# The first 13 rows of an output weight come in six loads by partition instead of being part of one

## The chip, the cores and the metric

The kernel runs on one core of a Trainium2 chip. The time is the device time of one execution in microseconds (us); lower is better. The kernel before takes 183.64 us, the median of three runs (183.59 to 183.73). The profile is of one execution more, which took 183.48 us.

A core has four computing engines, each with its own program: TensorE (PE in the profile), VectorE (DVE), ScalarE (ACT) and GpSimd (POOL). SyncE (SP) here issues nearly all transfers. A transfer between HBM, the chip's large memory, and SBUF, the working memory of 128 partitions, is carried by up to sixteen DMA engines; each of them works through its own queue in order and adds one to the transfer's semaphore when its share has landed. TensorE writes its sums to PSUM.

## The reference

The kernel computes one step of attention for 32 sequences with a cache, and the output projection:

```python
W = min(4096, max(256, Sk // 4))          # 512 of 2048 cached positions
rep = Hq // Hkv                           # 32 query heads, 8 cached heads: 4
q = (x @ wq).reshape(B, Sq, Hq, Dh).transpose(0, 2, 1, 3)
k = jnp.repeat(k_cache[:, :, Sk - W:, :], rep, axis=1)
v = jnp.repeat(v_cache[:, :, Sk - W:, :], rep, axis=1)
scores = jnp.einsum("bhqd,bhkd->bhqk", q, k) * (Dh ** -0.5)
p = _softmax(scores, axis=-1)
o = jnp.einsum("bhqk,bhkd->bhqd", p, v)
return o.transpose(0, 2, 1, 3).reshape(B, Sq, Hq * Dh) @ wo
```

Here B is 32, D is 512, Dh is 128 and Sq is 1; all values are bf16. The last product has a left side of 32 by 4096 and takes wo, 4096 by 512, which is 4 MiB.

## The kernel before, in words

The 32 sequences are taken four at a time, in eight groups (q = 0 to 7). A group's keys and values are 4 MiB each, so with wq and wo the kernel loads 18 times 4 MiB, and a little x. All the loads of 4 MiB or of its pieces are issued by SP in the order of the list `LOADS`: K is a group's keys, V a group's values (V5 to V7 in two pieces), W a part of wo. SP issues a load as soon as the buffer it fills is free: it waits on the counters that the engines raise after each operation (`op_sem`). The loads then stand in the queues of the DMA engines in that order. wq is issued ahead of the list (L203) and x by ScalarE (L199), in loads of 25, 5 and 2 rows (`X_PARTS`).

For each group VectorE turns the keys (L506, the buffer `K_sb` to `KT_sb`), TensorE forms the scores (`scores`, L341), VectorE and ScalarE the softmax, TensorE the transposed weights (`to_value_rows`, L355) and the products with the values (`pv`, L367), and `fold` (L377) with a copy by ScalarE (L566) puts a group's result in `o_sel`. The order of operations on each engine is written out by hand (`HEAD_OPS`, `BODY_OPS`, `TAIL_OPS`), and TensorE runs the middle as a loop. The two key buffers and the two value buffers alternate.

wo is loaded last, into the first key buffer, which is free once the keys of group 6 are turned (SP's wait for `ends["T", NQ - 2, 1]`). `wo_sb` has 128 partitions of 32 rows: partition p holds the rows 32 p to 32 p + 31 of wo, 512 values each, 1 KiB a row. `WOP` cuts the 32 rows into three loads, each over all 128 partitions: rows 0 to 21 (2816 KB), 22 to 29 (1024 KB) and 30 to 31 (256 KB). Every load has its own semaphore `sem_wo[j]`.

At the end TensorE waits until the results of all groups are in `o_sel`, then for one part of wo after another, and multiplies: four small multiplications per row (L462), 128 in all, into one bank of PSUM. VectorE (L548) and ScalarE (L602) copy the two halves of the sum to SBUF, and SP and ScalarE store one half each (L228).

## Time and profile before

| What | us |
|---|---|
| median of the runs | 183.64 |
| the profiled execution | 183.48 |
| its span, first to last instruction | 182.16 |
| DMA on the chain that ended last | 65% of the span |
| of it wo | 13.1% of the span |
| TensorE busy | 117.9 |
| VectorE busy | 109.0 |
| ScalarE busy | 46.6 |
| issue of the three loads of wo on SP | 154.73 to 156.28 |
| issue to landing of a load of wo, median | 22.0, 23.8 and 24.0 |

How to read it. The span is cut from the first to the last instruction; the execution's time has 1.32 us more around it. L with a number is a line of the kernel. A line of the chain or the timeline starts with the time from the span's start and the duration, both in us; PEld is the loading of TensorE's weights, and an engine's name with a q is its sequencer, which issues transfers. In brackets is the idle time ahead and what ended it. In the table of windows each engine has its busy time and the number of its instructions; after them come TensorE's granted clock, the mean busy share of the sixteen DMA engines, and what they moved in GB/s. The trace also holds, for each packet that a DMA engine carried, its start, duration, size and queue, and, for each semaphore, the times at which the DMA engines added to it. It doesn't name the DMA engine of a packet.

### The profile page before, as it was taken

What the parts mean: (1) busy time and instruction counts of PE and PEld (TensorE: products, weight loads), DVE (VectorE), ACT (ScalarE), POOL (GpSimd) and SP (SyncE); (2) the same over time, 40 slices, a digit from 0 to 9 for tenths busy, and PEclk for the clock granted to TensorE, in tenths of its full rate; (3) what the DMA queues carried; (4) which work ended last, traced back from release to release, by engine and by line L of the source; (5) the groups of instructions that cost most, each with busy time, mean ns of one, the idle gap of its engine ahead of it and who ended that gap; (6) DMA issues with size and microseconds to landing.
All of it is one profiled execution on the core that took longest, in us unless ns stands there. A gap on an engine that the chain in (4) does not pass through costs nothing.

```text
span 182.2 us, 3848 instructions
## 1 busy us (share of the span) xinstructions
PE 117.9 (65%) x1636; PEld 56.6 (31%) x1636; DVE 109.0 (60%) x103; ACT 46.6 (26%) x85; POOL 12.6 (7%) x34
## 2 busy tenths in 40 slices
PE   0029900444499669428993799344299699899954
PEld 0013400013035245105350345013044344454533
DVE  0022279939959960997079815997943699623030
ACT  3000220015116225402062016202007416354030
POOL 7500003000030000003000000012000000000000
PEclk9999975555579999975699579855579999999999
DMA  6998999899999999999999999999998999999991
GB/s 236 462 439 374 453 460 446 374 446 461 450 389 425 457 446 407 410 461 439 407 417 457 425 425 417 460 425 425 417 460 381 435 425 432 434 425 421 456 373 68
DMA packets 3459, 75.68 MB, mean 415 GB/s; under 512 B 412, under 2 KB 508, under 8 KB 636
## 3 DMA queue, kind: packets, MB, share of 16 engines
q1 hardware_dynamic: 3360, 75.52, 96.8%
q8 instruction: 7, 0.11, 0.3%
q10 hardware_dynamic: 92, 0.05, 0.2%
HBM read 75.53 MB, written 0.03 MB: 415 GB/s over the span
## 4 chain that ended last, share of the span: by engine, by line
DMA 65%; DVE 14%; PE 9%; issue 8%; SPq 1%; DVEq 1%; ACT 1%; ACTq 0%
DMA K_sb<-in_k_cache_dram 29%; DMA V_sb<-in_v_cache_dram 16%; DMA K_sb<-in_wo_dram 13%; DVE KT_sb L506 11%; DMA V_sb<-in_wq_dram 7%; PE ps L329 5%; PE ps L367 2%; DVE QT_sb L494 2%; PE ps L341 1%; SPq L253 1%; ACT KT_sb L556 1%; PE ps L462 1%; DVE maxv L520 0%; SPq L261 0%; SPq L246 0%
## 5 line engine op out<-in xcount | busy, mean ns | idle before, releaser
L506 DVE STREAM_TRANSPOSE KT_sb<-K_sb 128x4096 f32<-128x4096 f32 x16 | 70.2, 4424 | 16.2 <-DMA K_sb<-in_k_cache_dram 16.2
L367 PE MATMUL ps<-V_sb,bd 32*128 32x512 bf16 x1024 | 63.3, 398 | 8.0 <-DMA V_sb<-in_v_cache_dram 8.0
L341 PE MATMUL ps<-KT_sb,QBD 128*32 128x512 bf16 x256 | 22.3, 486 | 32.8 <-DVE KT_sb L506 32.8
L367 PEld LDWEIGHTS ps<-V_sb,bd 32*128 32x128 bf16 x1024 | 26.3, 98 | 40.5 <-DMA V_sb<-in_v_cache_dram 9.0
L587 ACT ACTIVATE bd<-PTc,mask 128x512 bf16 x32 | 20.5, 710 | 1.5 <-ACT PTc L582 1.5
L341 PEld LDWEIGHTS ps<-KT_sb,QBD 128*32 128x32 bf16 x256 | 6.3, 108 | 46.4 <-DVE KT_sb L506 38.3
L573 ACT ACTIVATE P_f<-ps,negmax 128x512 f32<-128x512 f32 x8 | 5.5, 687 | 54.1 <-DVE negmax L522 54.1
L377 PE MATMUL ps<-C_sb,F_pad 128*128 128x128 f32 x64 | 12.0, 345 | 5.3 <-DVE C_sb L518 3.7
L582 ACT ACTIVATE PTc<-ps 128x512 bf16<-128x512 f32 x8 | 4.8, 597 | 36.8 <-PE ps L355 36.8
L307 POOL COPY QBD<-QT_sb 32x256 bf16<-32x256 bf16 x16 | 6.3, 396 | 105.3 <-PE ps L341 89.3
L377 PEld LDWEIGHTS ps<-C_sb,F_pad 128*128 128x128 f32 x64 | 10.2, 242 | 10.3 <-DVE C_sb L518 7.9
L539 DVE TENSOR_SCALAR bd<-PTc,mask 128x512 bf16 x32 | 8.9, 346 | 6.4 <-ACT PTc L582 6.4
L329 PE MATMUL ps<-V_sb,bd 128*128 128x512 bf16 x32 | 9.7, 476 | 2.2 <-DMA V_sb<-in_wq_dram 2.2
L355 PE MATMUL ps<-P_bf,E_sb 128*128 128x128 bf16 x128 | 9.4, 231 | 2.6 <-DVE P_bf L529 2.6
L594 ACT ACTIVATE C_sb<-ps 32x512 f32<-32x512 f32 x14 | 8.2, 588 | 8.2 <-PE ps L367 8.0
L518 DVE COPY C_sb<-ps 32x512 f32<-32x512 f32 x12 | 8.3, 693 | 2.9 <-PE ps L367 2.5
L355 PEld LDWEIGHTS ps<-P_bf,E_sb 128*128 128x128 bf16 x128 | 7.9, 104 | 6.5 <-DVE P_bf L529 3.5
L546 DVE COPY C_sb<-ps 32x512 f32<-32x512 f32 x4 | 2.8, 694 | 9.5 <-PE ps L367 9.5
L520 DVE TENSOR_REDUCE maxv<-ps 128x1 f32<-128x512 f32 x8 | 5.5, 692 | 3.6 <-PE ps L341 3.4
L318 PE MATMUL ps<-bd 32*128 32x128 bf16 x4 | 0.6, 298 | 10.4 <-DMA bd<-in_x_dram 10.4
L478 DVE CAST bd<-ps 128x512 bf16<-128x512 f32 x1 | 0.7, 691 | 11.0 <-PE ps L318 11.0
L489 DVE CAST KT_sb<-ps 128x1024 bf16<-128x1024 f32 x2 | 2.4, 1224 | 7.8 <-PE ps L329 7.8
(30 smaller groups left out, 34.7 us busy)
## 6 DMA issues: line engine op xcount, KB each, us to landing
K_sb<-in_k_cache_dram SPq DMA_DIRECT2D x8, 4096.0 KB, 22.3
V_sb<-in_v_cache_dram SPq DMA_DIRECT2D x5, 4096.0 KB, 27.1
V_sb<-in_v_cache_dram SPq DMA_DIRECT2D x4, 2048.0 KB, 22.0
V_sb<-in_wq_dram SPq DMA_DIRECT2D x1, 4096.0 KB, 12.3
K_sb<-in_wo_dram SPq DMA_DIRECT2D x1, 2816.0 KB, 22.0
V_sb<-in_v_cache_dram SPq DMA_DIRECT2D x1, 2304.0 KB, 14.2
V_sb<-in_v_cache_dram SPq DMA_DIRECT2D x1, 1792.0 KB, 15.9
K_sb<-in_wo_dram SPq DMA_DIRECT2D x1, 1024.0 KB, 23.8
```

The costliest lines, as they stand in the source:

```text
L307: pool.tensor_copy(QBD[pr].rearrange("p u a (h c) -> p u a h c", h=HKV).rearrange("p u (w t) h c -> p (u w) t h c", w=2)[:, :, :, :, 4 * b ...
L329: ins = pe.matmul(ps[:, n], lhsT=xT_sb[:, kt, :], rhs=wq_sb[:, kt, n * 512:(n + 1) * 512], start=kt == 0, stop=kt == DKT - 1, tile_positio ...
L341: ins = pe.matmul(S_ps[32 * c:32 * c + 32, :], lhsT=QBD[:, q % 2, 2 * w + t, c0:c0 + 32], rhs=KT_sb[:, w, :, KB * h:KB * h + KB, t], start ...
L355: ins = pe.matmul(EP_ps[:, e * R:(e + 1) * R], lhsT=window[:, KB - 1 - k:KB - 1 - k + P], rhs=P_bf[:, k * R:(k + 1) * R], start=k == 0, st ...
L367: ins = pe.matmul(sums_of(b, q), lhsT=bd[pr, q % 2, 4 * g:4 * g + 4].rearrange("p r h e -> p (r h e)"), rhs=V_sb[q % 2][pr, 512 * g:512 * ...
L377: ins = pe.matmul(folds(q), lhsT=F_sb[:, d].rearrange("p h d -> p (h d)"), rhs=C_sb[:, q // LAST, :, NI * d:NI * d + NI], start=d == 0, st ...
L506: dve.transpose(KT_sb[:, w].bitcast(F32).rearrange("p r c t -> p r (c t)"), K_sb[i].bitcast(F32).rearrange("p (r w c) -> p r w c", r=R, w= ...
L518: dve.tensor_copy(*pick_args(r)).then_inc(op_sem["ANY", "C"], 1)
L520: dve.tensor_reduce(maxv[:, :], S_ps, AX.X, ALU.max).then_inc(s["dve_m"], 1)
L539: ins = dve.tensor_scalar(bd[:, bass.ds(odd, 1), :, h, :].rearrange("p o r e -> p (o r) e"), PTc[:, :, :], mask[:, h:h + 1], None, op0=ALU ...
L587: ins = act.activation(bd[:, bass.ds(odd, 1), :, h, :].rearrange("p o r e -> p (o r) e"), PTc[:, :, :], ACTF.Copy, scale=mask[:, h:h + 1])
L594: act.activation(*pick_args(r), ACTF.Copy).then_inc(op_sem["ANY", "C"], 1)
```

## The change

The rows 0 to 21 of wo, one load before, become two parts: rows 0 to 12 and rows 13 to 21. The second is one load over 128 partitions like the others. The first 13 rows come as six loads, divided by partition: partitions 0 to 111, 112 to 116, 117 to 121, 122 to 126, and partition 127 twice. The two loads of partition 127 take its 13 KiB in 32 runs of 416 bytes, one the even and the other the odd runs, sixteen each. All six raise the semaphore of the first part, and TensorE waits for six times 16 there. The same values land in the same places; the source is now described as (partition, row and column).

```diff
 LOADS = """
-K0 K1 V0.0 K2 V1.0 K3 V2.0 K4 V3.0 K5 K6 V4.0 K7 V5.0 V5.1 V6.0 V6.1 V7.0 V7.1 W0 W1 W2
+K0 K1 V0.0 K2 V1.0 K3 V2.0 K4 V3.0 K5 K6 V4.0 K7 V5.0 V5.1 V6.0 V6.1 V7.0 V7.1 W0 W1 W2 W3
 """.split()
...
-WOP = [(0, 22), (22, 30), (30, 32)]
+WOP = [(0, 13), (13, 22), (22, 30), (30, 32)]
+WO_ROWS = [[(0, 112), (112, 117), (117, 122), (122, 127), (127, 128, 0), (127, 128, 1)]] + 3 * [[(0, 128)]]
...
-            wo_h = wo.rearrange("(h r) n -> h (r n)", r=DH)
-            wo_r = wo_h.rearrange("h (d m) -> h d m", d=4)
+            wo_p = wo.rearrange("(p i) n -> p (i n)", i=NI)
+            wo_f = wo_sb.rearrange("p i n -> p (i n)")
...
                     i0, i1 = WOP[q]
-                    sp.dma_start(
-                        wo_sb[:, i0:i1, :].rearrange("p i n -> p (i n)"),
-                        wo_r[:, :, i0 * D:i1 * D],
-                    ).then_inc(sem_wo[q], 16)
+                    for p0, p1, *half in WO_ROWS[q]:
+                        here = lambda t: t[p0:p1, i0 * D:i1 * D] if not half else t[
+                            p0:p1, i0 * D:i1 * D].rearrange(
+                                "p (a e c) -> p e a c", a=16, e=2)[:, half[0]]
+                        sp.dma_start(here(wo_f), here(wo_p)).then_inc(sem_wo[q], 16)
...
             for j, (i0, i1) in enumerate(WOP):
-                pe.wait_ge(sem_wo[j], 16)
+                pe.wait_ge(sem_wo[j], 16 * len(WO_ROWS[j]))
```

## The prediction

> **What bounds the kernel now.** I read the page first, then the chain in order of time, the timeline of the last 10 us, and a table of windows there. The page gives the bound: the load queue takes 96.8% of sixteen DMA engines and the chain is mostly transfers.

> ```profile
> span 182.2 us, 3848 instructions
> ...
> q1 hardware_dynamic: 3360, 75.52, 96.8%
> q8 instruction: 7, 0.11, 0.3%
> ...
> DMA 65%; DVE 14%; PE 9%; issue 8%; SPq 1%; DVEq 1%; ACT 1%; ACTq 0%
> ```

> The end of the chain shows which transfer matters: wo, then a short fixed tail.

> ```profile
> 154.73 0.60 SPq L261
> 155.32 0.04 issue
> 155.37 23.82 DMA K_sb<-in_wo_dram
> 179.18 0.04 issue
> 179.23 0.99 PE ps L462 x40
> 180.21 0.02 issue
> 180.24 0.27 ACT P_bf L602
> ```

> The timeline shows that TensorE's first 88 multiplications wait for ScalarE (o_sel, 176.87 to 177.15), not for wo; only the last 40 wait for wo.

> ```profile
> 176.87 0.28 ACT L566 ACTIVATE o_sel<-ps 128x128 bf16<-128x128 f32 x1 [1.17 <-PE ps L377]
> ...
> 177.20 1.41 PE L462 MATMUL ps<-K_sb,o_sel 128*32 128x128 bf16 x88 [0.37 <-ACT o_sel L566]
> 179.22 0.46 PEld L462 LDWEIGHTS ps<-K_sb,o_sel 128*32 128x32 bf16 x32 [0.79 <-DMA K_sb<-in_wo_dram]
> 179.23 0.92 PE L462 MATMUL ps<-K_sb,o_sel 128*32 128x128 bf16 x40 [0.62 <-DMA K_sb<-in_wo_dram]
> ```

> The windows hold the point of this case. Before 178 us the engines are full; then the share is 0.37, which is 6 of 16.

> ```profile
> 170.00:174.00 4.00, 4.00 (x64) 2.15 (x64) 0.00 (x0) 0.00 (x0) 0.00 (x0) 1.00 1.05 449
> ...
> 178.00:178.50 0.50, 0.50 (x44) 0.43 (x32) 0.00 (x0) 0.00 (x0) 0.00 (x0) 1.00 0.37 156
> ```

> The trace's packet records say the same one by one. I call a DMA engine a lane: its packets follow each other without a gap, so a lane can be followed by time. The last wo load ends on ten lanes between 177.49 and 177.96, and on six between 179.04 and 179.36; its completions arrive about 0.44 later, the last at 179.80. The six fell behind one by one: five packets of 16384 B on the instruction queue (48.8, 59.6, 71.7, 87.6, 97.2 us) and a sixth at 173.5, about 1.06 us each, put one lane each some 1.55 us behind for good. These fetches are of the program, which the change leaves almost alone, so I keep them where they are.

> **The change, part by part.** In the same records a packet of 22528 B takes a step of 836 ns on its lane, 8192 B 309, 2048 B 80: 0.0368 ns per byte and about 5 to 8 ns each, so 13312 B is 496 ns, 9216 B 345, 416 B 20; a completion word takes 6.

> Where the small loads go: x's load of 25 rows ran on five lanes, five rows each, its load of five on the same five lanes, and its load of two on two of these. So the three loads of five partitions all go to those same five lanes (call them the five), 112 is seven on each of sixteen, and sixteen pieces are one on each. That the last holds for one partition no record shows; if all 32 pieces fell on one lane that lane would pay 32 x 20 = 0.64 us. I take sixteen lanes, the largest count up to sixteen that divides, as 25, 5 and 2 did.

> Removed on every lane: eight packets of 22528, 8 x 836 = 6.69 us. Added on eleven lanes: 7 x 496 + 8 x 345 + 2 x 20 + three more words of 6 = 6.29, so -0.40. Added on the five: 10 x 496 + 8 x 345 + 40 + six more words = 7.80, so +1.11.

> Are the five among the six late lanes? Followed by time, four of them are early; the fifth ran exactly in step with another lane from 9.9 to 42 us, and one of these two took the fetch at 59.6. By the completion delays the fifth is rather the early one (its delay stood 14 ns above the shortest of the five in the x loads; the two candidates later stand 8 and 21 above). I take all five as early.

> If lanes don't disturb each other, the five end at 177.96 + 1.11 = 179.07 at the latest and the late ones at 179.36 - 0.40 = 178.96. The end moves from 179.36 to 179.07: -0.29.

> Do they disturb each other? Today each lane writes eight partitions of every 128-partition load at 32768 B in 1209 ns, 27.1 B/ns. No row shows eight partitions taking more than that. The change sends five lanes at once into 16 neighbouring partitions (112 to 127). Lower bound: nothing, as when x rows of 1024 B took 46 ns at 6 us among full loads, the same as at 1.9 us; but that is 1 KB at a time. Upper bound: all of it through one lane's stream, 16 x 13312 / 27.1 = 7.86 us in place of 3 x 0.496 + 0.04 = 1.53, or +6.3. The nearest row is the long load: eight partitions, one stream. Sixteen partitions are then two streams, 3.93 us in place of 1.53: +2.40 on the five. I take this: 177.96 + 1.11 + 2.40 = 181.47, against 179.36: **+2.11**.

> [...]

> The other edits. SP issues nine loads in place of three: timeline 154.73 to 156.28, 0.52 each, so six more are 3.1 us. Only the store of the result stands behind them (SP waits for it until 180.53), and their packets start after 167.7, since twelve us of loads are queued ahead; without that cover the 3.1 would be paid. The small loads' own first-packet delay lies under the same queue. TensorE gets one wait more, for 13 rows and then 9; the first wait is for all six loads, and behind it stand all 128 multiplications of L462 and behind those the two copies of the result. o_sel holds TensorE to 177.20 anyway, and undisturbed the first 22 rows land by about 176.5. With +2.40 they land near 178.8, but their 88 multiplications (1.41 us) still finish before the next rows, 8 x 309 = 2.47 us later. What follows the last landing, 182.16 - 179.80 = 2.36 us, is unchanged.

> Sum, against the profiled execution: 183.48 us, of which the span is 182.16 and 1.32 lie around it. 183.48 + 2.11 = 185.59; that execution stands 0.16 under the median 183.64, so the median should be **185.7**.

> **Rivals.** (1) On the other side: lanes don't share. The last end moves by -0.29 (-0.37 if the slowest of the five is the lane that ended at 177.88): 183.64 - 0.29 to 0.37 = 183.3. For it: the 46 ns of the x rows, and that 1.1 up on the early and 0.4 down on the late closes a lag of about 1.4. Against: no row has several lanes in neighbouring partitions for long. It decides if sharing costs the five less than 0.29 us, the way from 179.07 to 179.36. (2) No sharing, but the fifth lane is the late one: it ends at 179.23 + 1.11 = 180.34, +0.98, time 184.6. For it: the two lanes in step; against: the delays, and that the other known fetches missed the five. (3) Sharing harder than priced. If four neighbouring partitions share one stream and the small loads go in turn, the fullest group takes four, three and three packets (112 to 115; 117 to 119; 124 to 126): 10 x 0.496 = 4.96 in place of 1.49, so +3.47: 177.96 + 1.11 + 3.47 = 182.54, +3.18, time 186.8. For it: the stream of 27.1 that no row exceeds; against: the x rows again, and a lane may run ahead into the next group. At the upper bound it is 177.96 + 1.11 + 6.3 = 185.4, +6.0, time 189.6. (4) The change does not do what it says, the pieces of the last partition on one lane: an early lane takes 0.64 and hides it; a late one ends at 178.94 + 0.64 = 179.58, +0.2, at most 183.9.

> **How the numbers follow.** Sharing in any strength that slows: 0.55, with my price in its middle and its own range 183.9 to 187.5: of the 0.55, 0.18 is rival 3's turn of groups and 0.10 lies above 187.5. No sharing and five early lanes: 0.33. The fifth late without sharing: 0.08. The pieces on one lane or sharing that eats just the gain: 0.04. The range is 183.2 (the gain of 0.37 and the spread of 0.07 of the three runs) to 187.5; outside it are 0.10 above and some 0.04 below. A change under 0.2% (0.37 us) is about what a measurement of this kernel can't tell from none. The gain of rival 1, 0.29 to 0.37, ends just there, so I halve its chance: faster 0.17, same 0.16 + 0.04 = 0.20, slower 0.63.

> **What would show it.** In the windows after the last full stretch, the DMA share: if the forecast holds it falls to about 5 of 16 (0.31), for over 2 us, and the wo packets of 13312 B in partitions 112 to 127 take well over 496 ns, 3.93 / 3 = 1310 on average. If those packets take 496, rival 1 or 2 holds, and one lane ending 1.3 us after all others tells rival 2. In the timeline the 88 multiplications should come in two lots, the second after 178.8; that TensorE still waits for the last landing alone confirms the unchanged tail. Loads that start late after SP's issue would show the cover wrong. The forecast is wrong if DMA takes many lanes into one partition group at full rate, or if sharing is as strong as one stream for all.

## The result, and the profile after

The changed kernel takes 190.22 us (median of six runs, 189.2 to 190.33) against 183.66 (six runs, 183.56 to 183.77): 1.0344 times as long, 95% interval 1.032 to 1.0367, or 6.56 us more. The direction was forecast, the size was not: 185.7 with 187.5 as the upper end. The profiled execution took 189.60 us with a span of 188.2.

The end of the chain in order of time, changed kernel. It still runs through wo and the same short tail, but wo ends later:

```profile
154.86 0.59 SPq L266
...
157.83 0.59 SPq L266
158.46 26.43 DMA K_sb<-in_wo_dram
184.93 1.33 PE ps L464 x36
186.29 0.27 ACT P_bf L604
```

SP issues its nine loads by 159.4 us, as worked out, and nothing waits for that: the first packet of 13312 B starts at 167.66, at the end of the same queue. The table of windows says where the time is. The last two columns are the busy share of the DMA engines and GB/s. First the changed kernel:

```profile
168.00:172.00 4.00, 3.39 (x56) 1.99 (x52) 0.00 (x0) 0.00 (x0) 0.00 (x0) 1.00 1.02 252
172.00:176.00 4.00, 2.95 (x56) 1.22 (x48) 0.97 (x2) 0.97 (x2) 0.00 (x0) 1.00 1.09 201
176.00:180.00 4.00, 1.16 (x8) 0.97 (x8) 0.42 (x1) 0.75 (x3) 0.00 (x0) 0.85 0.85 209
```

and the same first two stretches of the kernel before:

```profile
168.00:172.00 4.00, 4.00 (x64) 2.33 (x60) 0.00 (x0) 0.00 (x0) 0.00 (x0) 1.00 1.00 430
172.00:176.00 4.00, 2.47 (x43) 1.14 (x35) 1.39 (x2) 1.45 (x3) 0.00 (x0) 1.00 0.92 387
```

The engines are as busy as before, and move little more than half as much. They aren't waiting for work; each packet takes longer. And the loss begins at 168 us, with the load of 112 partitions, not with the small loads. The packet records agree: the packets of 13312 B took 818 ns on average in the first microsecond already, and 834 to 909 in each one from 169.5 to 172.5. The longest, later, took 1781. Even the nine rows over 128 partitions, which the change leaves a plain load, took 568 ns a packet on average in place of some 350.

TensorE in the timeline of the changed kernel:

```profile
177.67 0.28 ACT L568 ACTIVATE o_sel<-ps 128x128 bf16<-128x128 f32 x1 [1.17 <-PE ps L379]
...
180.42 1.58 PE L464 MATMUL ps<-K_sb,o_sel 128*32 128x128 bf16 x52 [2.79 <-DMA K_sb<-in_wo_dram]
...
182.48 1.15 PE L464 MATMUL ps<-K_sb,o_sel 128*32 128x128 bf16 x36 [0.48 <-DMA K_sb<-in_wo_dram]
...
184.93 1.26 PE L464 MATMUL ps<-K_sb,o_sel 128*32 128x128 bf16 x40 [1.30 <-DMA K_sb<-in_wo_dram]
```

o_sel is ready at 177.95 and no longer decides: TensorE waits 2.79 us for the first 13 rows. The last completion of wo comes at 185.52, 5.72 later than before.

### The profile page after: what moved, and what is told of

Same layout as the page of the kernel before. It is cut to its first block, busy times and chain, and to the rows that moved or that the text cites. A ratio compares the mean times of both kernels' runs of the same rounds, so it can differ in the third digit from the quotient of the medians.

```text
span 188.2 us, 3854 instructions
## 1 busy us (share of the span) xinstructions
PE 119.3 (63%) x1636; PEld 57.9 (31%) x1636; DVE 108.9 (58%) x103; ACT 46.6 (25%) x85; POOL 12.6 (7%) x34
## 3 DMA queue, kind: packets, MB, share of 16 engines
q1 hardware_dynamic: 3582, 75.52, 97.0%
## 4 chain that ended last, share of the span: by engine, by line
DMA 64%; DVE 13%; PE 9%; issue 8%; SPq 3%; DVEq 1%; ACT 1%; ACTq 0%
DMA K_sb<-in_k_cache_dram 28%; DMA V_sb<-in_v_cache_dram 15%; DMA K_sb<-in_wo_dram 14%; DVE KT_sb L508 11%; DMA V_sb<-in_wq_dram 7%; PE ps L331 5%; PE ps L369 2%; DVE QT_sb L496 2%; SPq L266 2%; PE ps L343 1%; PE ps L464 1%; SPq L254 1%; ACT KT_sb L558 1%; DVE maxv L522 0%; SPq L247 0%
## 5 line engine op out<-in xcount | busy, mean ns | idle before, releaser
L464 PE MATMUL ps<-K_sb,o_sel 128*32 128x128 bf16 x128 | 4.0, 311 | 4.6 <-DMA K_sb<-in_wo_dram 4.6
```

The lines of the kernel that those rows point to most:

```text
L464: ins = pe.matmul(Y_ps[32 * c:32 * (c + 1), 0:P], lhsT=o_sel[:, i, 8:], rhs=wo_sb[:, i, n * P:(n + 1) * P], start=i == 0, stop=i == NI - 1 ...
```

## The experiments

Two theories stood first. P: DMA engines that write neighbouring partitions share one stream, 27.1 bytes per ns (the 32768 B in 1209 ns of one engine). S: each further load costs by itself, wherever it writes. The run alone tests P in a sharper form, a supposition here: 128 partitions would fall into sixteen groups of eight, each of four neighbours and the four 32 further on, and a group would have one stream.

**Rows only.** The cut in rows without the cut in partitions:

```diff
-WO_ROWS = [[(0, 112), (112, 117), (117, 122), (122, 127), (127, 128, 0), (127, 128, 1)]] + 3 * [[(0, 128)]]
+WO_ROWS = 4 * [[(0, 128)]]
```

> The cut in rows alone: 13, 9, 8 and 2 rows, each one load over all 128 partitions. Theory P (DMA engines that write neighbouring partitions share one stream of 27.1 bytes per ns): nothing shares, so the time of before, 183.5 to 183.9 us. Theory S (each further load costs by itself, whichever partitions it has; 6.56 us for six further loads, 1.1 each): one further load, 184.8 us.

183.62 us against 183.61, ratio 1.0004 (0.9995 to 1.0014). The 128 packets of 13312 B took 498 to 508 ns. Four loads instead of three cost nothing that can be measured, and the new form of the source neither. All of the 6.56 us belongs to the cut in partitions.

**Two parts.**

```diff
+WO_ROWS = [[(0, 112), (112, 128)]] + 3 * [[(0, 128)]]
```

> The first 13 rows as two loads, partitions 0 to 111 and 112 to 127. Theory P: the packets of the load of 112 take some 850 ns as in the changed kernel (7 x 0.35 = 2.5 us more than 496), and the load of 16 has sixteen engines on four groups of four neighbours, 16 x 13312 / (4 x 27.1) = 1.96 us in place of 0.50; together about 4 us, 187.6 us. Theory S: two loads more than before, 2.2 us, 185.9 us, with packets of 496 ns in the load of 112.

190.11 us, ratio 1.033 (1.0279 to 1.038). Both missed: P's 187.6 was too low and S's 185.9 further off. The number of small loads hardly matters: one load of 16 partitions costs what five did.

**The last partition in one load.**

```diff
+WO_ROWS = [[(0, 112), (112, 117), (117, 122), (122, 127), (127, 128)]] + 3 * [[(0, 128)]]
```

> The changed kernel with partition 127 as one load. Theory P: the pieces were 13 KB of the 213 KB for 16 partitions, so the time stays within 0.6 us of the changed kernel's 190.2, whichever way. Theory S: one load less, 189.1 us. If the pieces of 416 bytes were the cost themselves, it falls by several us.

190.16 us, ratio 1.036 (1.034 to 1.0381): as the changed kernel. The pieces of 416 B are not the cost, though in the changed kernel they took 45 ns on average.

**Loads alone.** Behind the end of the kernel before, one load at a time:

```diff
+            for where, cols in PROBE:
+                sp.dma_start(V_sb[0][where, 0:cols], wo_p[where, 0:cols]).then_inc(sem_t, 16)
+                n += 1
+                sp.wait_ge(sem_t, 16 * n)
```

> The kernel before, and behind its end loads of 32 rows of wo (32768 bytes a partition) into a free buffer, one at a time, each awaited; the time of the whole says nothing, the packets do. One engine alone should take about 1210 ns. Theory P, groups of four neighbours and the four 32 away: partitions 0 and 1: 2420 ns each; 0 and 4: 1210; 0 and 32: 2420; 0 and 64: 1210; 112 to 115: 4840; 112 to 116: four at 4840, the fifth 1210; 0, 4, 8, 12, 16: 1210; 112 to 127: 4840; every eighth partition: 2420; 0 to 63: 2420 on average; 0 to 111: about 1.7 x 1210 = 2060; 0 to 127: 1210. Theory S: 1210 everywhere.

The table is from the packet records and the completions. The packets' own times missed the expectation: a lone packet took 1812 ns, not 1210, and four neighbours 3134 to 3782, not 4840. For the four, the last packet ended 3.78 us after the first began, but the last data landed at 5.42. So the last column is compared instead. It holds about 0.9 us besides the transfer (2.11 for a lone packet, against 1.21 in the full stream).

```
partitions written      packets of 32768 B, ns   first packet to last completion, us
0                       1812                     2.11
0, 1                    2298, 2306               3.41
0, 4                    1909, 1944               2.24
0, 32                   1554, 2066               2.86
0, 64                   1661, 1774               2.07
112 to 115              3134 to 3782             5.42
112 to 116              2425; 3415 to 3629       5.46
0, 4, 8, 12, 16         1492 to 2094             2.41
112 to 127              3315 to 3758             5.36
0, 8, 16, ... 120       1792 to 2602             3.62
0 to 63                 mean 2518                11.40
0 to 111                mean 1920                14.83
0 to 127                mean 1292                11.20
```

**Crossed.** In the run alone, source and destination were of the same partitions, so the rows in HBM could be the ones that collide (theory H). Here they are chosen apart.

```diff
+                sp.dma_start(
+                    V_sb[0][slice(*where_to), 0:FULL], wo_p[slice(*where_from), 0:FULL]
+                ).then_inc(sem_t, 16)
```

> As in the run alone, loads of 32768 bytes a partition behind the end, one at a time, but source and destination chosen apart, each twice: the rows of wo that belong to partitions 0 and 1 go to partitions 0 and 4, and so on. Theory P (the destination partitions are shared): two engines to 0 and 1, or to 0 and 32, land about 1.2 us later than to 0 and 4, or 0 and 64, whatever the source rows; four engines to 112 to 115 land 3.6 us later than to 0, 4, 8, 12, also with the sources swapped. Theory H (the source rows in HBM collide): the time goes with the source rows instead, and to 0 and 4 from the rows of 0 and 1 it is as late as to 0 and 1.

```
rows of partitions   written to       first packet to last completion, us, two tries
0, 1                 0, 1             2.76  3.32
0, 4                 0, 4             2.16  1.93
0, 32                0, 32            2.75  3.20
0, 64                0, 64            1.88  2.03
0, 1                 0, 4             2.24  2.17
0, 4                 0, 1             2.75  3.05
0, 64                0, 1             3.22  3.01
0, 1                 0, 64            1.89  1.65
112 to 115           0, 4, 8, 12      2.29  2.16
0, 4, 8, 12          112 to 115       5.26  5.14
```

For these loads of two and four partitions the destination decides and the source doesn't (rows of 0, 4, 8, 12 to 112 to 115: 5.26 and 5.14 us, the other way round 2.29 and 2.16): H is out here. 0 and 32 are as late as 0 and 1 (2.75 and 3.20 against 2.76 and 3.32). The load of 112 partitions wasn't run crossed, so for it a part of the source is not excluded.

**Which part costs how much.** Now within P: is it the load of 112 (P1) or the small loads (P2)? The load of 112 alone:

```diff
+WO_ROWS = [[(0, 112)]] + 3 * [[(0, 128)]]
```

> Leaves out the first 13 rows of partitions 112 to 127, so no small load is left: the load of 112 partitions, then 9, 8 and 2 rows over 128. Theory P1 (the load of 112 itself is the larger cost, because seven consecutive partitions per engine do not line up with groups of four, so engines meet in a group; alone it took 14.8 us where 128 took 11.2): packets of about 850 ns, and 183.6 + 7 x 0.35 - 0.5 = 185.6 us or more, up to 188. Theory P2 (the small loads are the cost, as the prediction had it): packets of 496 ns and 183.2 us, one packet less per engine.

187.43 us against 183.54, ratio 1.0214 (1.0197 to 1.0231): 3.89 us more, with an eighth of these rows left out. Its packets took 837 ns on average, and those of the nine rows behind them 492. P1's time and packets came as expected, so the load of 112 is slow without any small load. P1's reason isn't shown by it (below). Windows of this run:

```profile
168.00:172.00 4.00, 3.70 (x60) 2.05 (x56) 0.14 (x1) 0.00 (x0) 0.00 (x0) 1.00 1.05 269
```

The small loads alone, added to loads of 128:

```diff
+WO_ROWS = 4 * [[(0, 128)]]
+MORE = [(112, 117), (117, 122), (122, 127)]
...
+                        for j, where in enumerate(MORE):
+                            where = slice(*where)
+                            sp.dma_start(
+                                K_sb[1][where, COL[j]:COL[j] + 13 * D],
+                                wo_p[where, 0:13 * D]).then_inc(sem_more, 16)
```

> All of wo in loads over 128 partitions (13, 9, 8, 2 rows), and three loads more of five partitions, 112 to 116, 117 to 121, 122 to 126, 13 rows each, into the free second key buffer, ahead of the nine rows. 200 KB more in 16 partitions. P1: these loads cost less than the load of 112: under 2 us, 184 to 185.6 us. P2: the priced +1.1 + 2.4 less the lag of 1.4 that the five engines have in hand, plus what the owners of these groups lose, 185.7 to 187.5 us. If lanes do not share at all: 183.8 (1.5 us more on five engines, 1.4 in hand).

187.1 us, ratio 1.0188 (1.0171 to 1.0205): 3.56 more, in P2's range and above P1's. So both theories hold half: neither part is small. The two don't add up (3.89 + 3.56 = 7.45 against 6.56), as one run leaves rows out and the other adds 200 KB. The same loads on partitions that don't neighbour:

```diff
-MORE = [(112, 117), (117, 122), (122, 127)]
+MORE = [(0, 20, 4), (64, 84, 4), (20, 40, 4)]
```

> The same three loads of five partitions, same engines, sizes and place in the queue, but every fourth partition (0 to 16, 64 to 80, 20 to 36), so that the five engines of a load write five different groups. Theory P (1 or 2): each of these packets shares with the one engine that owns the group, so about 2 x 496 ns at first, and less is lost than in the near form: 183.8 to 185.2 us, and 0.5 us or more under the near form. Theory S (each small load costs by itself): the same as the near form within 0.2 us.

184.65 us, ratio 1.0062 (1.0045 to 1.0078): 1.11 more. Same bytes, same number of loads, five partitions each; which partitions they are makes 2.45 us. The windows, first the near form, then the far:

```profile
168.00:172.00 4.00, 4.00 (x68) 2.31 (x63) 0.00 (x0) 0.00 (x0) 0.00 (x0) 1.00 1.04 426
172.00:176.00 4.00, 2.48 (x44) 1.19 (x36) 1.39 (x2) 1.45 (x3) 0.00 (x0) 1.00 1.03 145
```

```profile
168.00:172.00 4.00, 4.00 (x65) 2.32 (x60) 0.00 (x0) 0.00 (x0) 0.00 (x0) 1.00 1.01 426
172.00:176.00 4.00, 2.48 (x45) 1.06 (x38) 1.39 (x2) 1.45 (x3) 0.00 (x0) 1.00 1.00 326
```

Up to 172 us, while the loads of 128 run, all is as before; then 145 GB/s against 326. In the far form 15 packets of 13312 B are over 600 ns, as many as were added, 822 on average: by P, each shares with the one engine whose group it is. In the near form 27 are over 600, 1388 on average: more than were added, so packets of the load of 128 beside them were slowed too.

**Halves.** A cut that P can price without any small load. The first 13 rows come as two loads, partitions 0 to 63 and 64 to 127; by P each lies in eight of the sixteen groups, so that sixteen engines are two to a group on average and a packet takes 2 x 496 ns:

```diff
+WO_ROWS = [[(0, 64), (64, 128)]] + 3 * [[(0, 128)]]
```

> [...] Theory P: packets of 992 ns, 8 x 0.496 = 4.0 us more: 187.6 us. Theory S: one load more than in the run with rows only, about 184.8 us, with packets of 496 ns.

190.02 us, ratio 1.0372 (1.034 to 1.0404): 6.5 more, where P said 4.0 and S 1.2.

```profile
168.00:172.00 4.00, 3.05 (x48) 1.85 (x44) 0.00 (x0) 0.00 (x0) 0.00 (x0) 1.00 1.00 209
172.00:176.00 4.00, 3.14 (x56) 1.30 (x56) 0.78 (x2) 0.78 (x2) 0.00 (x0) 1.00 0.98 212
```

Both times were too low. But the packets of 13312 B took 980 ns on average, as P has it (992), and 8 x (980 - 502) = 3.8 us. Most of the rest is in the loads ahead and behind: the eight packets of 14336 B before (595 ns against 539, 0.4 us) and the eight of nine rows (529 against 354, 1.4 us). Together that is 5.7 of the 5.88 us by which the last landing moved. Why these loads were slowed too is not shown.

## Why the prediction was right or wrong

- **The sum of undisturbed packets** was right where nothing is shared: 13312 B take 502 ns (496 said), 9216 B 354 with a median of 348 (345 said).
- **What failed first: "Added on eleven lanes: 7 x 496".** The load of 112 was costed as undisturbed, and sharing was looked for only in partitions 112 to 127. Its packets took 837 ns with no small load near, and were slow from the first microsecond. By itself this load costs 3.89 us, where the prediction had -0.40 for these lanes. Why it is slow stays open (below).
- **What failed second: "8 x 345" behind it.** The nine rows were also taken as undisturbed; they took 568. Summed per engine from the changed kernel's packets: (578 - 539) x 8 = 0.3 us in the last load of values, and 127 x 953 / 16 + 8 x 568 = 12.1 us for the first 22 rows, where the run with rows only has 8 x 502 + 8 x 354 = 6.8. That is 5.6 of the 5.72 us by which the last landing moved.
- **The small loads** were priced by eight partitions to a stream, +2.40. In the run alone four neighbours are late by 3.3 us, 0 and 32 by 0.75, 0 and 4 by 0.13, and 16 neighbours are no later than four (5.36 against 5.42): the partitions that share aren't eight neighbours there. The near form gave 3.56, which is near rival 3's turn of groups (+3.18) rather than the forecast (+2.11), though it adds bytes that the change does not. An even filling of four streams, an estimate from the 27.1 bytes per ns, is 16 x 13312 / (4 x 27.1) = 1.96 us in place of 1.53, +0.43: far too low. That the direction came true was not luck: the small loads do slow each other in neighbouring partitions, as forecast, by the 2.45 us between near and far.
- **The bound above** (189.6, everything through one stream) was no bound, for it left out the load of 112.
- **The tail "is unchanged"** was wrong by a little: from the last landing to the end of the span it is 188.2 - 185.52 = 2.68 us in place of 2.36 (below).
- **SP's issue, the wait of TensorE and o_sel**: nothing of the time went there, but o_sel no longer covers the first rows. The 88 multiplications came in two lots as foretold, at 180.42 and 182.48; any slowing of the first 13 rows would have brought that.
- **Rival 1** (no sharing) and **rival 4** (pieces on one lane) are out. The pieces came as sixteen packets a load, and behind the run alone each of two such loads landed in sixteen separate increments of its semaphore. Whether the fifth lane is one of the late ones (**rival 2**) was not settled; it came to matter for nothing here.
- **"The DMA share falls to 5 of 16 for over 2 us"** did not come: most engines were slowed together (the packets of 13312 B took 953 ns on average) and the share stayed at 0.85 to 1.09 in the three windows from 168 to 180 us. GB/s, not the share, showed the loss.

More than that, the idea of taking work from the late engines may have no gain to give here. By P a late engine's group of partitions has one stream, which its own packets already fill while they run; other engines that help would only share it, as by P the 15 packets of the far form did (822 ns on average against 502). This is argued: no run shifted work in another way.

One thing stays open, and it is the cause of the largest term: why the packets of 112 take 1.7 times as long. P1 has it that each engine takes seven consecutive partitions, so that engines meet in a group. No record shows which partitions an engine has. The halves don't settle it, for by P partitions 0 to 63 lie in only eight of the sixteen groups, and twice the time follows from more than one division. And an estimate speaks against P1 as the whole reason. With seven consecutive partitions each, the groups of P and all sixteen engines in step, two or four of them share a group at each step, never more than two in one. That makes 1.21 times the 496 ns of an undisturbed packet, about 600 ns, where the run of 112 alone had 837. In the run behind the end no packet of 112 took under 1331 ns, while most of 128 took 1211 to 1213: nearly all were slowed, not a few pairs. A part of the source rows remains possible too.

## What to carry to other kernels

Loads that keep all sixteen DMA engines busy can still run at little more than half the rate (252 GB/s against 430 here): compare GB/s, not the busy share, stage by stage. Cut a large load along the bytes of a partition (that cost nothing here: 183.62 us against 183.61), and not along the partitions: of the large loads tried, 128 at once was the only form that kept its rate (packets of 13312 B at 502 ns; 837 in the load of 112 alone, 980 in the halves). Before shifting work between engines, ask which resource behind the engine is full; where it belongs to the destination, other engines may not add to it: here four engines that wrote 112 to 115 landed 3.3 us after a lone one.

## What the runs showed that was not expected

- 112 partitions alone took 14.83 us where 128 took 11.20, and 64 took 11.40: fewer bytes, not less time.
- The slowing reached the load behind as well: in the run without small loads, the plain packets of nine rows were 492 ns instead of 354.
- TensorE's granted clock fell during its wait. The windows of the changed kernel (the third last column is the granted clock):

```profile
178.00:180.00 2.00, 0.00 (x0) 0.00 (x0) 0.00 (x0) 0.00 (x0) 0.00 (x0) 0.69 0.90 274
180.00:182.00 2.00, 1.58 (x52) 1.34 (x52) 0.00 (x0) 0.00 (x0) 0.00 (x0) 0.50 1.02 420
184.00:186.00 2.00, 1.07 (x40) 0.99 (x40) 0.00 (x0) 0.00 (x0) 0.00 (x0) 0.50 0.16 60
```

It was idle from 177.63 to 180.42, and the last 40 multiplications took 1.26 us at a granted clock of 0.50, where they took 0.92 at 1.00 before. That is the 0.3 us by which the tail grew.
